# Seven block products for eight in the output projection of a fused attention and feed-forward kernel

## The chip, the cores and the metric

The kernel runs on one core of a Trainium2 chip. The metric is the device time of one execution in microseconds, from 2 runs of the kernel before: 248.40 and 248.44 us, median 248.42 us. Five engines work side by side, each with its own instruction queue that it executes in order: PE (TensorE, matrix products; its weight loads are listed apart as PEld), DVE (VectorE), ACT (ScalarE), POOL (GpSimd) and SP (SyncE, which here only issues DMAs). An instruction that needs another engine's result waits on a semaphore, and all that stands behind it in the queue of its engine waits with it. Matrix products are written to PSUM; PE, DVE and ACT work there, POOL works in SBUF only.

## The reference

There are 8 batches (`B`), 8 heads, 576 positions, head size 64, and 32 packed queries. First the packed queries attend to the keys and values, then the positions attend to the result; the outcome goes through a feed-forward layer whose activation is `h * cos(h)`:

```python
p_packed = sm_attn(p, k, v)
out = sm_attn(q, p_packed, p_packed)
x = attn_out.transpose(0, 2, 1, 3).reshape(B * S, H * D)    # 4608 x 512
h = x @ w_in                                                # 512 x 2048
g = h * np.cos(h)
return g @ w_out                                            # 2048 x 512, float32
```

`sm_attn` is a softmax attention. All products are taken in bf16 with fp32 sums in PSUM; `out` is fp32.

## The kernel before, in words

The program is written out by hand in one order for each engine; no planner moves anything. A tile pool hands out a free buffer when a tile is made in the program, and the first writer of the buffer waits until the last reader of its former tile has finished. Two PSUM pools matter: `psA` (three buffers of two banks, pool `A`) and `ot` (two buffers of one bank, pool `O`).

The work of batch s is split into a **front** and a **slot**.

- The front of s has the second attention of s: scores and their exponentials (`s2`), the second half of the product of the packed values and `w_in` (`ppw`, parts 2 and 3; DVE casts them from `psA` to the SBUF tile `PPW`), the softmax sums by a product with a block of ones (`sums2`, followed by a logarithm on ACT) and `normalise`, which takes the exponential of minus that logarithm on ACT and multiplies on DVE into the bf16 tile `a2n`. It has also the first scores of batch s+1 (`s1`).
- The slot of s makes the hidden layer in 16 steps (`h_mm(s, fc)`, fc = 0 to 15). Each step has four products of 288 columns on PE (L256) into a `psA` buffer, the cosine on ACT (L260) and the multiplication on DVE (L263), which writes 128 rows of `gT[s]`. At some steps hooks are called: `pp(s+1)` (L183) needs the permuted values `vp`, which POOL makes with one copy for each batch (`permute_v`), and `a1T`, which a transposing DMA on SP's queue brings; `pw2(s+1)` makes the first two parts of `PPW` of the next batch.
- Between all of this `fill(n)` puts n products of the **output projection of batch s-1**. Each product has one 128 x 128 block of `gT` as its weights and 512 columns of `w_out` (L309). 16 of them make a chunk of 128 positions in one `ot` buffer; a copy then brings it to SBUF (`osb`: on DVE in the fronts, on ACT in the slots) and SP issues its stores. 576 positions are four chunks and a half. The last 64 positions of two neighbouring batches are copied by POOL into the tile `joint` (L267) and make one more chunk. In the front of s, 32 products are put between the steps; the slot spreads the rest over its 16 steps and keeps 5 for the beginning of the next front.

Batches 0, 1 and 2 have fronts of their own (L366 to L505), and from 3 on there is one loop (L507). After the slot of batch 7, the output projection of batch 7 follows alone (L542, L543) and at last the joint chunk of batches 6 and 7 in two halves of 256 columns (`tail_chunk`, L295).

POOL's queue in the steady part of a batch has the two `joint` copies, `permute_v`, a tiny copy that waits for a transposed tile (`gate`, L527), and the issue of the loads of `v`, `q` and `k` of later batches. SP's queue has the stores of the chunks and the transposing DMAs of `q`, `a1` and `k`.

Of the kernel before, what the change touches and what calls it, by code (L numbers as in the profile page):

```python
# [8 lines left out]
FP32 = mybir.dt.float32  # L9
BF16 = mybir.dt.bfloat16  # L10
# [5 lines left out]
def kernel(  # L16
# [10 lines left out]
    nc = tc.nc  # L27
    B, H, S, D = q.shape
# [5 lines left out]
    TP = S // C  # L34
    HS = S // 2
# [4 lines left out]
    const = ctx.enter_context(tc.tile_pool(name="const", bufs=1))  # L40
    bf_pool = ctx.enter_context(tc.tile_pool(name="bf", bufs=1))
    vp_pool = ctx.enter_context(tc.tile_pool(name="vp", bufs=2))
    att_pool = ctx.enter_context(tc.tile_pool(name="att", bufs=1))
    a2n_pool = ctx.enter_context(tc.tile_pool(name="a2n", bufs=2))
    ppw_pool = ctx.enter_context(tc.tile_pool(name="ppw", bufs=2))
    g_pool = ctx.enter_context(tc.tile_pool(name="g", bufs=2))
    j_pool = ctx.enter_context(tc.tile_pool(name="joint", bufs=2))
    cos_pool = ctx.enter_context(tc.tile_pool(name="cos", bufs=3))
    o_pool = ctx.enter_context(tc.tile_pool(name="o", bufs=4))
# [8 lines left out]
    w_out_bf = const.tile([128, NFC, DM], BF16, name="w_out_bf")  # L58
    ident = const.tile([128, 128], BF16, name="ident")
# [3 lines left out]
    p_raw = const.tile([128, 2 * B, D], FP32, name="p_raw")  # L63
# [131 lines left out]
    def ppw(b, n, eng=None, own=False, later=False, cuts=((0, 512),)):  # L195
        if b not in PPW:
            PPW[b] = ppw_pool.tile([128, 2, DF], BF16, name="PPW", tag="PPW")
# [12 lines left out]
        def evacuate(cuts=cuts):  # L210
            if own or two:
                for a, z in cuts:
                    for y in range(2):
                        copy(eng[y] if two else eng, PPW[b][:, y, n * 512 + a:n * 512 + z], ps[y][:, a:z])
            else:
                copy(eng or (V, ACT)[n % 2], PPW[b][:, :, n * 512:(n + 1) * 512], t)
# [4 lines left out]
    def s2(b):  # L221
        a2u[b] = att_pool.tile([128, 2, S], BF16, name="a2u", tag="a2u")
# [5 lines left out]
    def sums2(b, y):  # L228
        if b not in lns:
            lns[b] = att_pool.tile([128, 2, S], FP32, name="lns", tag="lns")  # L230
        ps = psa()
        for e in range(2):
            nc.tensor.matmul(ps[:, e, 0:HS], ones_blk, a2u[b][:, y, e * HS:(e + 1) * HS],  # L233
                             start=True, stop=True)
        ACT.activation(out=lns[b][:, y].rearrange("p (e x) -> p e x", e=2),  # L235
                       in_=ps[:, :, 0:HS], func=AF.Ln)

    def normalise(b):
        a2n[b] = a2n_pool.tile([128, 2, S], BF16, name="a2n", tag="a2n")
        for y in range(2):  # L240
            ACT.activation(out=lns[b][:, y], in_=lns[b][:, y], func=AF.Exp, scale=-1.0)  # L241
        for y in range(2):
            V.scalar_tensor_tensor(out=a2n[b][:, y], in0=a2u[b][:, y], scalar=r1[b][:, y:y + 1],  # L243
# [331 lines left out]
```

The softmax here doesn't subtract the row's maximum and nothing guards it: scores larger than these inputs give would overflow.

## Time and profile before

| | |
|---|---|
| median of 2 runs | 248.42 us (248.40 to 248.44) |
| profiled execution, its own time | 248.62 us |
| its span, first to last instruction | 246.8 us |
| granted TensorE clock | 1.000 |
| PE, DVE, ACT, POOL busy | 233.2, 165.2, 169.0, 57.7 us |
| hidden layer on DVE (L263), 128 times | 93.8 us, 755 ns each |
| products of the output projection (L309), 128x512 | 127.5 us and 12.8 us (joint chunks) |
| DMA, mean | 151 GB/s, 37.36 MB in packets |

The span is 1.8 us shorter than the profiled execution's time, since a part of the start and the end lies outside the first and the last instruction. In the rows of groups the second number is the mean duration of one instruction. Products are pipelined on PE: the listed 379 ns of one product of 512 columns is from its first to its last effect, and the next one starts earlier; how many fit into a stretch is seen in the rows of the timeline, which merge instructions of one kind (start, duration, engine, line, operation, count).

### The profile page before, as it was taken

The numbers are of one execution on the slowest core, as the hardware profiler recorded it, in microseconds if no ns is written. First come the engines' busy times: TensorE is split into PE (matmuls) and PEld (weight loads), VectorE is DVE, ScalarE is ACT, GpSimd is POOL, SyncE is SP. The second block draws the span as 40 slices with busy tenths as digits, with TensorE's granted clock in tenths as the row PEclk, the third lists the DMA queues.
The fourth block names the chain that finished last, engine by engine and source line by source line (L and its number), as shares of the span: only waits on it lengthen the run. The fifth ranks groups of instructions, "written<-read, shape, count | busy, mean of one in ns | idle before, by whom it ended". The sixth has DMA issues, their size and how long they took to land.

```text
span 246.8 us, 5023 instructions
## 1 busy us (share of the span) xinstructions
PE 233.2 (94%) x1996; PEld 130.9 (53%) x2029; DVE 165.2 (67%) x248; ACT 169.0 (68%) x282; POOL 57.7 (23%) x70
## 2 busy tenths in 40 slices
PE   8788799999999999999999999999999999999993
PEld 3454374566545654565446554565456554665452
DVE  3549987677658776678767766678766684886110
ACT  2369799877576787888787776888778684873000
POOL 8342533240400355004503105030500100001000
PEclk9999999999999999999999999999999999999999
DMA  6999999999899999999999997999571113111133
GB/s 90 202 203 206 205 206 228 194 241 151 179 202 184 192 175 214 218 198 142 222 211 187 172 201 91 198 166 171 109 154 27 45 43 84 43 31 57 47 84 85
DMA packets 64231, 37.36 MB, mean 151 GB/s; under 512 B 36848, under 2 KB 59632, under 8 KB 64208
## 3 DMA queue, kind: packets, MB, share of 16 engines
q0 software_dynamic: 23152, 18.75, 50.0%
q1 hardware_dynamic: 40624, 18.09, 35.1%
q8 instruction: 16, 0.26, 0.4%
q10 hardware_dynamic: 432, 0.20, 0.4%
q14 instruction: 7, 0.06, 0.1%
HBM read 37.22 MB, written 9.44 MB: 189 GB/s over the span
## 4 chain that ended last, share of the span: by engine, by line
PE 78%; DMA 12%; issue 2%; DVE 2%; ACT 2%; POOL 2%; DVEq 0%; POOLq 0%
PE ot L309 46%; PE psA L256 21%; DMA vbf<-in_v_dram 10%; PE psA L207 3%; DMA a1T<-a 2%; PE psA L129 2%; PE psA L183 2%; DVE gT L263 2%; PE ot L295 1%; PE psA L233 1%; ACT cosT L260 1%; POOL vp L77 1%; ACT ppT L75 1%; POOL kbf L84 1%; PE ot L104 0%
## 5 line engine op out<-in xcount | busy, mean ns | idle before, releaser
L309 PE MATMUL ot<-w_out_bf,gT 128*128 128x512 bf16 x482 | 127.5, 379 | 2.0 <-issue 1.1
L263 DVE TENSOR_TENSOR gT<-psA,cosT 128x576 bf16<-128x576 f32 x128 | 93.8, 755 | 28.9 <-ACT cosT L260 28.2
L260 ACT ACTIVATE cosT<-psA 128x576 bf16<-128x576 f32 x128 | 82.4, 652 | 24.6 <-PE psA L256 22.1
L256 PE MATMUL psA<-a2n,PPW 128*128 128x288 bf16 x512 | 83.8, 286 | 1.6 <-DVE gT L263 0.4
L309 PEld LDWEIGHTS <-gT 128*128 128x128 bf16 x512 | 47.8, 98 | 43.4 <-issue 6.7
L256 PEld LDWEIGHTS <-PPW 128*128 128x128 bf16 x512 | 49.3, 98 | 34.6 <-issue 3.9
L77 DVE CAST PPW<-psA 128x1024 bf16<-128x1024 f32 (+1 forms) x23 | 26.9, 1175 | 11.6 <-PE psA L207 11.5
L267 POOL COPY joint<-gT 128x512 bf16<-128x512 bf16 x16 | 9.9, 616 | 82.5 <-DVE gT L263 82.5
L77 DVE COPY osb<-ot 128x512 f32<-128x512 f32 (+1 forms) x22 | 14.9, 678 | 17.5 <-PE ot L309 7.7
L77 POOL COPY vp<-vbf 96x3072 bf16<-96x3072 bf16 x7 | 19.3, 2751 | 6.3 <-DMA vbf<-in_v_dram 6.3
L75 ACT COPY osb<-ot 128x512 f32<-128x512 f32 (+1 forms) x15 | 8.5, 567 | 15.3 <-PE ot L309 10.6
L243 DVE SCALAR_TENSOR_TENSOR a2n<-a2u,r,lns 128x576 bf16<-128x576 bf16 x16 | 12.3, 812 | 7.3 <-ACT lns L241 7.3
L235 ACT ACTIVATE lns<-psA 128x576 f32<-128x576 f32 x16 | 10.1, 650 | 7.1 <-PE psA L233 6.5
L140 ACT ACTIVATE a<-psA 128x576 bf16<-128x576 f32 x16 | 10.3, 647 | 6.7 <-PE psA L129 6.7
L309 PE MATMUL ot<-w_out_bf,joint 128*128 128x512 bf16 x47 | 12.8, 379 | 0.1
L225 ACT ACTIVATE a2u<-psA,rs 128x576 bf16<-128x576 f32 x16 | 11.0, 737 | 1.4 <-PE psA L129 1.3
L75 ACT CAST ppT<-psA 64x128 bf16<-64x128 f32 x24 | 6.2, 260 | 7.0 <-DVE ppT L77 5.9
L207 PE MATMUL psA<-w_in_bf,ppT 64*32 64x512 bf16 x224 | 10.1, 380 | 0.0
L241 ACT ACTIVATE lns<-lns 128x576 f32<-128x576 f32 x16 | 10.0, 676 | 0.0
L347 PE MATMUL ot<-wz 128*128 128x512 bf16 x23 | 7.7, 468 | 1.4 <-DVE wz L358 1.2
L527 POOL COPY gate<-kT 1x1 bf16<-1x1 bf16 x3 | 0.5, 181 | 32.3 <-DMA kT<-kbf 32.3
L183 PEld LDWEIGHTS <-vp 96*128 96x128 bf16 x192 | 6.5, 98 | 2.3 <-issue 1.2
(73 smaller groups left out, 152.7 us busy)
## 6 DMA issues: line engine op xcount, KB each, us to landing
kbf<-in_k_dram POOLq DMA_DIRECT2D x8, 576.0 KB, 12.6
vbf<-in_v_dram POOLq DMA_DIRECT2D x8, 576.0 KB, 7.6
qbf<-in_q_dram POOLq DMA_DIRECT2D x8, 576.0 KB, 10.1
out_dram<-osb SPq DMA_DIRECT2D x24, 192.0 KB, 2.7
out_dram<-osb SPq DMA_DIRECT2D x22, 128.0 KB, 2.4
w_in_bf<-in_moe_w_in_dram POOLq DMA_DIRECT2D x4, 512.0 KB, 17.3
w_out_bf<-in_moe_w_out_dram POOLq DMA_DIRECT2D x4, 512.0 KB, 21.2
out_dram<-osb SPq DMA_DIRECT2D x26, 64.0 KB, 2.1
```

Source lines behind the costliest of these rows:

```text
L75: ACT.copy(out=out, in_=in_)
L77: eng.tensor_copy(out=out, in_=in_)
L140: ACT.activation(out=a1[b % 2][:, y, :, 0:TP].rearrange("p (e m) x -> p e m x", e=2), in_=ps[y][:, :, 0:HS].rearrange("p e (m x) -> p e m ...
L183: nc.tensor.matmul(ps[:, hp * 64:(hp + 1) * 64], vp[b][:, c, hp * 128:(hp + 1) * 128], a1T[b][0:TP, :, j, 32 * hp:32 * hp + 32], start=(j ...
L207: nc.tensor.matmul(ps[y][32 * x:32 * x + 32, :], ppT[b % 2][r, 2 * x + y, :], w_in_bf[r, x, n * 512:(n + 1) * 512], start=True, stop=True)
L225: ACT.activation(out=a2u[b][:, y].rearrange("p (e x) -> p e x", e=2), in_=ps[y][:, :, 0:HS], func=AF.Exp, scale=rs1[b][:, y:y + 1])
L235: ACT.activation(out=lns[b][:, y].rearrange("p (e x) -> p e x", e=2), in_=ps[:, :, 0:HS], func=AF.Ln)
L243: V.scalar_tensor_tensor(out=a2n[b][:, y], in0=a2u[b][:, y], scalar=r1[b][:, y:y + 1], in1=lns[b][:, y], op0=ALU.mult, op1=ALU.mult)
L256: nc.tensor.matmul(ps[:, e, 0:HS], PPW[b][:, y, fc * 128:(fc + 1) * 128], a2n[b][:, y, e * HS:(e + 1) * HS], start=(y == 0), stop=(y == 1))
L260: ACT.activation(out=csv, in_=ps[:, :, 0:HS], func=AF.Sin, bias=PI_HALF)
L263: V.tensor_tensor(out=gT[b][:, fc, :].rearrange("p (e x) -> p e x", e=2), in0=ps[:, :, 0:HS], in1=csv, op=ALU.mult)
L309: nc.tensor.matmul(pss[c], w, w_out_bf[:, fc, :], start=(fc == 0), stop=(fc == NFC - 1))
```

## The change

The output projection of batches 1 to 7 is made differently. Chunks 2 and 3 are made as before, one after the other, and now come first, in the fronts. Chunks 0 and 1, 256 positions together, are made as one block product of 2 x 2 blocks (`pair_gen`): the rows in two blocks of 128 positions, the inner dimension in two halves (even and odd steps fc), the columns in two halves of 256. The eight block products are replaced by seven, with sums of blocks ahead of and behind them (the scheme of Strassen and Winograd). Each of the seven has 8 products of 256 columns, so a pair has 56 products of 256 columns for 32 of 512.

- **Sums ahead.** Four sums of blocks of `w_out` (`T_sums`, made once, on POOL, in and after slot 1) and four sums of blocks of `gT` for each batch (`S_sums`, made in two halves of 4 steps, so 8 instructions of 128x512 elements). These stand on POOL's queue at the beginning of the front of s for batch s-1 (`close`), ahead of `permute_v(s+1)`; for batch 1 one half of them stands behind `permute_v(3)`, and for batch 7 they are on DVE.
- **Sums behind.** The seven products come in five groups, each in one `ot` buffer: (1), (2, 6), (7), (4, 5), (3). ACT or DVE copies the first to SBUF, and DVE makes five additions for each pair (`plus`), of 512, 256, 512, 256 and 256 columns, from PSUM and SBUF to SBUF.
- **Joint chunks** are made in halves of 256 columns; for batches 3 to 6 one half goes with each batch.
- `fill` counts in halves: a product of 256 columns is one, a product of 512 columns is two. A slot keeps 10 halves for the next front: the last two of products (4, 5) and the eight of product 3.
- **`normalise`** works in PSUM: `sums2` writes the logarithm back to its `psA` buffer, the exponential stays there too, and DVE reads it from there; the two buffers are held until then. From batch 2 on the two multiplications of `normalise` are not put at once: the first one comes after `fill(7)`, the second after `fill(3)` more.
- Room in SBUF: `vp` has one buffer for two, `PPW` four tiles of 512 columns for two of 2048, `p_raw` shares its place with the fourth sum of `w_out`, and the tile `lns` is gone.

```diff
-    vp_pool = ctx.enter_context(tc.tile_pool(name="vp", bufs=2))
+    vp_pool = ctx.enter_context(tc.tile_pool(name="vp", bufs=1))
-    ppw_pool = ctx.enter_context(tc.tile_pool(name="ppw", bufs=2))
+    ppw_pool = ctx.enter_context(tc.tile_pool(name="ppw", bufs=4))
+    u_pool = ctx.enter_context(tc.tile_pool(name="u", bufs=2))
+    T = [const.tile([128, 8, 256], BF16, name=f"T{i}") for i in range(3)]
...
     def sums2(b, y):
-        if b not in lns:
-            lns[b] = att_pool.tile([128, 2, S], FP32, name="lns", tag="lns")
-        ps = psa()
+        ps = lns[b, y] = psa()
...
-        ACT.activation(out=lns[b][:, y].rearrange("p (e x) -> p e x", e=2),
-                       in_=ps[:, :, 0:HS], func=AF.Ln)
+        ACT.activation(out=ps[:, :, 0:HS], in_=ps[:, :, 0:HS], func=AF.Ln)
...
+    def normalise(b, later=False):
+        a2n[b] = a2n_pool.tile([128, 2, SQ], BF16, name="a2n", tag="a2n")
+        for y in range(2):
+            t = lns[b, y][:, :, 0:HS]
+            ACT.activation(out=t, in_=t, func=AF.Exp, scale=-1.0)
+
+        def product(y):
+            v = [t[b][:, y].rearrange("p (e x) -> p e x", e=2) for t in (a2n, a2u)]
+            V.scalar_tensor_tensor(out=v[0], in0=v[1], scalar=r1[b][:, y:y + 1],
+                                   in1=lns[b, y][:, :, 0:HS], op0=ALU.mult, op1=ALU.mult)
+        if later:
+            return product
+        product(0)
+        product(1)
...
+    def A_blk(b, m, odd, k0, k1):
+        return gT[b][:, 2 * k0 + odd:2 * k1:2, m * 128:(m + 1) * 128]
+
+    def B_blk(odd, n):
+        return w_out_bf[:, odd:NFC:2, n * 256:(n + 1) * 256]
+
+    def T_sums(i, eng):
+        if i == 3:
+            T.append(s_pool.tile([128, 8, 256], BF16, name="T3", tag="x"))
+        in0, in1 = ((B_blk(0, 1), B_blk(0, 0)), (B_blk(1, 1), T[0]), (B_blk(1, 1), B_blk(0, 1)), (B_blk(1, 0), T[1]))[i]
+        eng.tensor_tensor(out=T[i], in0=in0, in1=in1, op=ALU.subtract)
...
+    def S_sums(b, p, eng, k0, k1, which=(0, 1, 2, 3)):
+        if (b, p) not in S:
+            S[b, p] = s_pool.tile([128, 4, 8, 128], BF16, name=f"S{p}", tag=f"S{p}")
+        t = S[b, p]
+        A11, A12 = (A_blk(b, 2 * p, i, k0, k1) for i in range(2))
+        A21, A22 = (A_blk(b, 2 * p + 1, i, k0, k1) for i in range(2))
+        S1, S2, S3, S4 = (t[:, i, k0:k1, :] for i in range(4))
+        for i in which:
+            out, in0, in1, op = ((S1, A21, A22, ALU.add), (S2, S1, A11, ALU.subtract),
+                                 (S3, A11, A21, ALU.subtract), (S4, A12, S2, ALU.subtract))[i]
+            eng.tensor_tensor(out=out, in0=in0, in1=in1, op=op)
...
+    def pair_gen(b, p):
...
+        A11, A12 = (A_blk(b, 2 * p, i, 0, 8) for i in range(2))
+        S1, S2, S3, S4 = (S[b, p][:, i] for i in range(4))
+        o1 = o_pool.tile([128, 3, 256], FP32, name="osb1", bufs=2)
+        o2 = o_pool.tile([128, 2, 256], FP32, name="osb")
+        m1, u3 = (u_pool.tile([128, 256], FP32, name=n, tag=n) for n in ("m1", "u3"))
+        m = {1: (A11, B_blk(0, 0)), 2: (A12, B_blk(1, 0)), 3: (S4, B_blk(1, 1)),
+             4: (A_blk(b, 2 * p + 1, 1, 0, 8), T[3]), 5: (S1, T[0]), 6: (S2, T[1]), 7: (S3, T[2])}
+
+        def then_double(ps):
+            plus(o2, ps, u3)
+            store(o2, 2 * p + 1)
+            plus(o1[:, 2], ps[:, 1], o1[:, 2])
+
+        def then_last(ps):
+            plus(o1[:, 1], ps, o1[:, 2])
+            store(o1, 2 * p)
+
+        then = {1: lambda ps: copy(out_eng[0], m1, ps), 2: lambda ps: plus(o1[:, 0:3:2, :], ps, m1),
+                7: lambda ps: plus(u3, ps, o1[:, 2]), 4: then_double, 3: then_last}
+
+        for names in ((1,), (2, 6), (7,), (4, 5), (3,)):
+            ps = O.tile([128, 2, 256], FP32, name="ot", tag="ot")
+            for i, n in enumerate(names):
+                lhs, rhs = m[n]
+                for kp in range(8):
+                    nc.tensor.matmul(ps[:, i], lhs[:, kp, :], rhs[:, kp, :], start=kp == 0, stop=kp == 7)
+                    if kp == 7 and n == names[-1]:
+                        then[names[0]](ps if i else ps[:, 0])
+                    yield 1
...
+    def out_gen(b):
+        for j, i in joints_of(b):
+            yield from joint_half(j, i, store_half(j))
+        if b == 0:
+            yield from direct_gen(b, ((0, 1), (2,), (3,)))
+        else:
+            yield from direct_gen(b, ((2,), (3,)))
+            yield from pair_gen(b, 0)
...
+    def close(s, groups=(0, 4)):
+        fill(1000)
+        for k0 in groups:
+            S_sums(s, 0, V if s == B - 1 else G, k0, k0 + 4)
+        set_filler(s)
...
-    slot(1, [(3, lambda: pw2(1, 2, (ACT, V))), (4, lambda: (xbar("q", 2), xbar("k", 3))), (5, tk("k", 2, 0)), (6, tk("k", 2, 1)),
-             (7, tk("k", 2, 2)), (9, lambda: pack_p(2, 4)), (12, next_loads)], 4, {3: 3})
+    slot(1, [(1, lambda: (T_sums(0, G), T_sums(1, G))), (3, lambda: pw2(1, 2, (ACT, V))), (4, lambda: (xbar("q", 2), xbar("k", 3))), (5, tk("k", 2, 0)), (6, tk("k", 2, 1)),
+             (7, tk("k", 2, 2)), (9, lambda: pack_p(2, 4)),
+             (12, next_loads)], 8, {3: 3})
+    T_sums(2, G)
+    T_sums(3, G)
...
-    fill(1000)
-    set_filler(1)
+    close(1, (0,))
...
-    normalise(2)
+    product = normalise(2, later=True)
     ACT.preload_act_table_set(SIN_SET)
-    fill(8)
+    fill(7)
+    product(0)
+    fill(3)
+    product(1)
     G.tensor_copy(out=gate, in_=a2n[2][0:1, 1, 0:1])
     permute_v(3)
+    S_sums(1, 0, G, 4, 8)
...
-        fill(1000)
-        set_filler(s - 1)
+        close(s - 1)
         if nxt:
             permute_v(s + 1)
...
-        normalise(s)
+        product = normalise(s, later=True)
         ACT.preload_act_table_set(SIN_SET)
-        fill(13)
+        fill(7)
+        product(0)
+        fill(3)
+        product(1)
+        fill(3)
...
-        slot(s, [(5, lambda: pp(s + 1, engs=(ACT, ACT))), (10, lambda: pw2(s + 1))] if nxt else [], 5, {10: 3})
-    out_eng[:] = V, ACT
-    set_filler(B - 1)
+        slot(s, [(5, lambda: pp(s + 1, engs=(ACT, ACT))), (10, lambda: pw2(s + 1))] if nxt else [], 10, {10: 3})
+    close(B - 1)
     fill(1000)
-    tail_chunk(B - 1, 4)
+    tail_chunk(B - 1)
```

## The prediction

> **What bounds the kernel now.** I read the page's busy shares and slices first, then the timeline of one batch, then the timeline of the places where the changed program holds a buffer longer. In the slices a 9 means 90% or more.
>
> ```profile
> PE 233.2 (94%) x1996; PEld 130.9 (53%) x2029; DVE 165.2 (67%) x248; ACT 169.0 (68%) x282; POOL 57.7 (23%) x70
> ...
> PE   8788799999999999999999999999999999999993
> ```
>
> From the seventh slice (some 37 us) on PE is full until the end. In a slot a step takes four products of L256 (0.49 us) and one or two of L309, and the next step follows at once: 129.86, 130.78, 131.70 for steps with two. So a product taken from PE there shortens the run by its full time, and every wait put ahead of PE lengthens it as directly, since PE's queue passes nothing.
>
> The rate of the two product sizes stands at the end of the timeline, where PE runs the last batch alone:
>
> ```profile
> 223.84 15.27 PE L309 MATMUL ot<-w_out_bf,gT 128*128 128x512 bf16 x69
> ...
> 239.16 3.66 PE L295 MATMUL ot<-w_out_bf,joint 128*128 128x256 bf16 x32
> ```
>
> From 223.84 to 239.16 are 71 products by the program (7 left over, 64 of batch 7; two records are missing): 215.8 ns each. The 32 of 256 columns take 3.66 us with 0.27 for the last one's full duration: (3.66 - 0.27)/31 = 109.3 ns. Half the columns cost half the time.
>
> **What goes from PE.** A pair of chunks was 32 x 215.8 = 6.91 us and becomes 56 x 109.3 = 6.12. Over 7 batches: -5.49 us. Three joint chunks become 32 x 109.3 for 16 x 215.8: +0.13. Net **-5.36 us**; the hidden layer and the attention keep their products.
>
> **What is added on DVE, and the price of its rows.** Per pair five additions from PSUM. The trace has no such addition; the nearest rows are the osb copy of 512 columns (690 ns), of 256 columns (424 ns), and the multiplication with one PSUM and one SBUF input of 576 columns (755 ns, 0.70 when back to back). I take 0.69 and 0.42: 2.6 us per pair, where before two ACT copies stood. A slot had 16 x 0.755 + 1.22 (cast of PPW) = 13.3 us of DVE in 15 to 19 us; only 1.1 us of the additions (2, 6 and 7) fall into it, so DVE isn't the bound by throughput. What counts is whom an addition keeps waiting.
>
> **(a) Front boundary.** One boundary in the timeline of before:
>
> ```profile
> 146.78 1.89 PE L309 MATMUL ot<-w_out_bf,joint 128*128 128x512 bf16 x8
> ...
> 147.66 0.76 DVE L263 TENSOR_TENSOR gT<-psA,cosT 128x576 bf16<-128x576 f32 x1 [0.16 <-ACT cosT L260]
> ...
> 148.70 0.69 DVE L77 COPY osb<-ot 128x512 f32<-128x512 f32 x1 [0.29 <-PE ot L309]
> ...
> 149.18 2.33 PE L309 MATMUL ot<-w_out_bf,gT 128*128 128x512 bf16 x9
> ```
>
> The last step's products end at 146.78 (call it t0). The last multiplication ends at t0 + 1.64. Before, the next chunk (149.18, t0 + 2.40) took the other `ot` buffer, long free. Now both are taken, by (4, 5) and (3). That of (4, 5) is free after two additions queued behind the last multiplication: 1.64 + 0.69 + 0.42 and some 0.05 for the semaphore = t0 + 2.80. PE gets there at 14 x 0.109 = 1.53, plus 0.68 for the scores and the part of `ppw` in between (148.50 to 149.18): t0 + 2.21. PE waits 0.6 us, ahead of fronts 3 to 7: **+3.0** (bounds: 0.3 each if the additions take half a copy, 0.9 if the slot ends with DVE late). Ahead of batch 7's own projection nothing covers: 2.80 - 1.53 = **+1.3**.
>
> **(b) Start of the slots.** The first step needs both halves of `a2n`.
>
> ```profile
> 154.48 2.97 PE L309 MATMUL ot<-w_out_bf,gT 128*128 128x512 bf16 x12
> ...
> 155.93 1.55 DVE L243 SCALAR_TENSOR_TENSOR a2n<-a2u,r,lns 128x576 bf16<-128x576 bf16 x2 [1.46 <-ACT lns L241]
> ...
> 157.28 0.65 PE L256 MATMUL psA<-a2n,PPW 128*128 128x288 bf16 x4
> ```
>
> `a2n` was whole at 157.48, PE came to the second half at 157.53: no slack at all. In the changed order of batches 4 to 7 (16 halves of a joint chunk first) chunk 2 ends 10 halves behind the last `sums2`, and its copy stands ahead of the first multiplication on DVE: 154.48 + 1.09 + 0.2 = 155.77, copy to 156.46, multiplications to 157.24 and 158.01. PE waits 0.5 to 0.6 there: **+2.2** for four batches (0 if DVE reads PSUM that much faster, 0.8 each if slower). In front 3 the copy falls elsewhere, and nothing is lost.
>
> **(c) `psA` held by `normalise`.** Two of the three buffers stay with the logarithms until the multiplications.
>
> ```profile
> 18.08 1.48 DVE L77 COPY kT<-psA 128x768 bf16<-128x768 bf16 x3 [1.40 <-PE psA L104]
> ...
> 19.49 1.53 DVE L243 SCALAR_TENSOR_TENSOR a2n<-a2u,r,lns 128x576 bf16<-128x576 bf16 x2
> ...
> 22.64 1.19 ACT L260 ACTIVATE cosT<-psA 128x576 bf16<-128x576 f32 x2
> ```
>
> At the start three groups of transposes (0.47 us each) filled three buffers; now they share one, each behind the copy of the one before: copies end at 18.6, 19.7, 20.9, the multiplications start 1.4 us later, and half of the scores of batch 1 wait for the first. The first cosine comes about 1.9 later. DVE has no gap up to 31.5 and then 0.53, 0.33 and 0.24 us of them to win back: **+0.8** (0 to 1.9). In front 2 two parts of `ppw` follow each other:
>
> ```profile
> 73.55 0.63 PE L207 MATMUL psA<-w_in_bf,ppT 64*32 64x512 bf16 x16
> ...
> 74.03 2.35 DVE L77 CAST PPW<-psA 128x1024 bf16<-128x1024 f32 x2 [1.16 <-PE psA L207]
> ```
>
> One free buffer: the second part waits for the first cast, 1.2 + 0.3 = 1.5 us on PE. The 0.38 us that PE waits for `a1T` at 84.43 goes: **+1.1** (0.7 to 1.9).
>
> **(d) Inside the slots** two additions stand between multiplications, and a `psA` buffer comes free up to 0.7 later. With steps of 0.85 us (62 halves in a slot) that is nearly covered: 0.1 each in slots 4 to 7; in slots 2 and 3 (48 and 46 halves, steps of 0.76, as long as a multiplication) 0.3 each: **+1.0** (0 to 4). **(e) The end:** (4, 5) waits 0.2 for the addition behind (2, 6), the last joint half 0.55 for the two behind (4, 5): **+0.75**.
>
> **(f) POOL.** No sum of two inputs by POOL is in the trace. Its copies of 512 and 3072 elements take 0.616 and 2.751 us: 0.19 + 0.834 ns per element. A sum of 512 costs 0.62 if the second input is free, 1.04 if it counts as one more element, 2.1 as upper end (twice that). I take 1.04, nearest to the copies.
>
> ```profile
> 148.48 0.61 POOL L267 COPY joint<-gT 128x512 bf16<-128x512 bf16 x1 [9.36 <-DVE gT L263]
> ...
> 149.03 2.75 POOL L77 COPY vp<-vbf 96x3072 bf16<-96x3072 bf16 x1
> ```
>
> Eight sums now stand between these two rows. `pp`, which needs `vp`, came at 161.80, 13.3 us behind the joint copy; with (a) and (b) 14.5. 0.61 + 8 x 1.04 + 2.75 = 11.7: in time. Above 1.39 us per sum `vp` is late. The sums of `w_out` (0.19 + 4096 x 0.834 ns = 3.6 us each) fit into POOL's waits of 9.1 and 9.6 us in slot 1 and front 2. Loads and the queue of SP shift by under 1 us: **0**. The last batch's sums on DVE (8 below 0.75) end ahead of product 6, 11 us behind t0.
>
> [...]
>
> **Sum.** -5.36 + 3.0 + 1.3 + 2.2 + 0.8 + 1.1 + 1.0 + 0.75 = **+4.8 us**. Profiled execution 248.62 + 4.8 = 253.4; it was 0.2 above the median, so **253.2 us**. 2% of 248.42 (5.0 us) is about what a measurement can tell from no change; this lies beside it.
>
> **Rivals.** *The waits are covered* (22%): the additions are short, products and multiplications slide into place, and of the losses only the two in (c) remain: 248.4 - 5.4 + 1.9 = 245; with half of (a), (b), (d), (e) 249. For it: DVE has a third of the span idle. Against it: each wait is a place in one queue, not a share. *POOL comes late* (15%): from 1.39 us per sum on, each 0.1 more makes `pp` wait 8 x 0.1 in fronts 3 to 6, 3.2 us in all; at 1.6 it is 6.7 us, 260; at 2.1 it is 23 us, 276. For it: two inputs through an engine which copies at 0.83 ns per element. Against: 23% busy. *The seven products don't run at half time* (8%) between products of 288 columns with other weights: at 120 ns for 109, 56 x 7 x 0.011 = 4.3 us, 257.5.
>
> **How the numbers follow.** My forecast (55%) runs from 249 to 257.5 with its terms' bounds. The range 246.5 to 259 leaves out the bottom of the first rival (8%) and the top of POOL's (11%). Faster by over 2% (below 243.4) needs all waits covered: 4%. Slower by over 2% (above 253.4) is the forecast's upper half and the last two rivals: 50%. Same: 46%.
>
> **What would show it.** Right: PE busy falls by about 5 us while its idle time grows by 10; PE waits of 0.6 us for DVE at the first `ot` product of fronts 3 to 7 and 1.3 ahead of batch 7; 0.5 at the start of slots 4 to 7; 1.5 in front 2; the first cosine near 24.5. Wrong: `pp` waiting for POOL's `vp`, POOL sums above 1.4 us, products of 256 above 112 ns, or PE full throughout.

## The result and the profile after

The changed kernel takes **257.88 us** (257.21 and 258.56) against 248.42 before: 1.038 times as long, with a 95% interval of 1.026 to 1.050. The profiled execution took 257.21 us, with a span of 255.4 us, 8.6 us more than before in both.

The page's lines on busy time and the slices, as they answer to those of the kernel before (PEclk is the granted clock of TensorE in tenths):

```profile
PE 233.0 (91%) x2226; PEld 153.2 (60%) x2245; DVE 185.7 (73%) x284; ACT 167.9 (66%) x285; POOL 127.6 (50%) x122
...
PE   8777589999997999999999999999999999998993
...
PEclk9999979999999999999999999999999999999999
```

PE has as much busy time as before, though its work fell by 5.4 us (reckoned from the rates of the two product sizes). The slices say where to look: a 5 in the fifth, followed by a sixth at a lower clock. That is stage 0, from 25 to 38 us. I call the moment at which a slot's last hidden-layer products end, and PE goes on to the next row of the timeline, the end of the slot. Its time, us, with the difference below:

| | slot 0 | slot 1 | slot 2 | slot 7 | span |
|---|---|---|---|---|---|
| before | 36.85 | 61.60 | 93.35 | 223.84 | 246.8 |
| after | 41.70 | 66.73 | 99.75 | 231.45 | 255.4 |
| later by | 4.85 | 5.13 | 6.40 | 7.61 | 8.6 |

More than half of the loss is there before the first slot ends, ahead of every block product. The rows of the timeline of the changed kernel in that place (start, duration, engine, line, operation, count, and in brackets the idle time before it and what ended it):

```profile
24.63 1.19 ACT L266 ACTIVATE cosT<-psA 128x576 bf16<-128x576 f32 x2
...
28.31 0.78 POOL L87 DMA_DIRECT2D kbf<-in_k_dram  x1 [1.87 <-DMA vbf<-in_v_dram]
...
28.77 3.10 DVE L155 TENSOR_SCALAR rs<-r 128x2 f32<-128x2 f32 x1
...
29.09 2.76 POOL L80 COPY vp<-vbf 96x3072 bf16<-96x3072 bf16 x1
...
32.58 1.93 PE L262 MATMUL psA<-a2n,PPW 128*128 128x288 bf16 x8 [2.94 <-DVE gT L269]
```

The first cosine comes at 24.63, 1.99 late. Then DVE spends 3.10 us on `rs`, the product of two numbers per partition with a constant, and its row ends with POOL's copy of `vp` (29.09 + 2.76 = 31.85). Behind `rs` stand the multiplications, PE's three `psA` buffers are full, and PE waits 2.94 us. Its clock falls after that, as the answer by stretches shows (length, busy time of PE, PEld, DVE, ACT and POOL with the instructions in brackets, granted clock, share and GB/s of the DMA engines):

```profile
30.00:32.00 2.00, 0.00 (x0) 0.00 (x0) 2.00 (x2) 0.42 (x1) 1.84 (x1) 1.00 1.32 205
32.00:34.00 2.00, 1.40 (x7) 0.62 (x7) 2.00 (x4) 0.65 (x1) 0.78 (x1) 0.82 1.25 207
34.00:36.00 2.00, 2.00 (x15) 0.77 (x14) 1.89 (x4) 1.17 (x2) 0.61 (x1) 0.50 1.24 205
36.00:38.00 2.00, 2.00 (x34) 1.61 (x33) 1.66 (x3) 1.58 (x4) 0.00 (x0) 0.83 1.24 206
```

At half clock PE counts as busy and gets less done: eight products of the hidden layer from 35.00 took 1.97 us, where eight from 30.70 took 1.16 before the change. So a lost 2.94 us became more, and the busy sum of PE hides it. In the groups by line, `rs` is a line that I had not read before:

```profile
L155 DVE TENSOR_SCALAR rs<-r 128x2 f32<-128x2 f32 x8 | 10.1, 1260 | 0.3
```

In the kernel before the same group (L152) had 1.8 us in 8 instructions, 231 ns each.

The waits that the prediction did name are there, all a little shorter. From timelines of the changed kernel: front 2, the front and the slot of batch 5, and the last batch.

```profile
80.94 0.41 PE L209 MATMUL psA<-w_in_bf,ppT 64*32 64x512 bf16 x8 [1.35 <-DVE PPW L80]
...
155.00 1.91 PE L322 MATMUL ot<-w_out_bf,joint 128*128 128x256 bf16 x16 [0.35 <-DVE osb L369]
...
163.77 0.41 PE L262 MATMUL psA<-a2n,PPW 128*128 128x288 bf16 x2 [0.26 <-DVE a2n L245]
...
234.08 7.08 PE L344 MATMUL ot<-w_out_bf,gT 128*128 128x512 bf16 x31 [0.94 <-DVE osb L369]
241.00 1.91 PE L396 MATMUL ot<-w_out_bf,gT 128*128 128x256 bf16 x16
242.74 1.91 PE L396 MATMUL ot<-T,S 128*128 128x256 bf16 x16
...
247.73 3.65 PE L322 MATMUL ot<-w_out_bf,joint 128*128 128x256 bf16 x32 [0.33 <-DVE osb L369]
```

The 16 products from 241.00 to 242.74 take 109 ns each. And POOL's sums, the first with 512 elements, the second (one of `w_out`) with 2048:

```profile
69.01 4.06 POOL L289 TENSOR_TENSOR T<-w_out_bf 128x2048 bf16<-128x2048 bf16 x1
...
78.28 1.15 POOL L303 TENSOR_TENSOR S<-S,gT 128x512 bf16<-128x512 bf16 x1
```

### The profile page after: what moved, and what is told of

Its sections match the earlier page's. It is cut to its first block, busy times and chain, and to the rows that moved or that the text cites. A ratio compares the mean times of both kernels' runs of the same rounds, so it can differ in the third digit from the quotient of the medians.

```text
span 255.4 us, 5593 instructions
## 1 busy us (share of the span) xinstructions
PE 233.0 (91%) x2226; PEld 153.2 (60%) x2245; DVE 185.7 (73%) x284; ACT 167.9 (66%) x285; POOL 127.6 (50%) x122
## 4 chain that ended last, share of the span: by engine, by line
PE 64%; DVE 16%; ACT 9%; issue 5%; DMA 4%; POOL 1%; DVEq 0%; ACTq 0%; POOLq 0%
PE ot L344 20%; PE psA L262 20%; PE ot L396 11%; DVE gT L269 6%; PE ot L322 5%; ACT cosT L266 5%; DMA qbf<-in_q_dram 4%; DVE osb L369 3%; DVE a2n L245 2%; PE psA L209 2%; ACT ppT L78 2%; PE psA L233 2%; PE psA L132 2%; DVE osb L80 1%; PE psA L107 1%
## 5 line engine op out<-in xcount | busy, mean ns | idle before, releaser
L344 PE MATMUL ot<-w_out_bf,gT 128*128 128x512 bf16 x271 | 70.2, 379 | 2.1 <-DVE osb L369 1.4
L303 POOL TENSOR_TENSOR S<-gT 128x512 bf16<-128x512 bf16 x24 | 27.7, 1152 | 0.0
L396 PE MATMUL ot<-T,S 128*128 128x256 bf16 x168 | 24.4, 273 | 0.0
L396 PEld LDWEIGHTS <-S 128*128 128x128 bf16 x224 | 21.5, 98 | 4.5 <-issue 1.4
L396 PE MATMUL ot<-w_out_bf,gT 128*128 128x256 bf16 x112 | 18.0, 273 | 0.0
L322 PE MATMUL ot<-w_out_bf,joint 128*128 128x256 bf16 x128 | 15.4, 272 | 1.8 <-DVE osb L369 1.8
L235 ACT ACTIVATE psA<-psA 128x576 f32<-128x576 f32 x16 | 10.0, 635 | 7.8 <-PE psA L233 3.8
L322 PEld LDWEIGHTS <-joint 128*128 128x128 bf16 x128 | 12.2, 98 | 4.8 <-issue 3.5
L303 POOL TENSOR_TENSOR S<-S,gT 128x512 bf16<-128x512 bf16 x12 | 13.8, 1151 | 0.9
L303 POOL TENSOR_TENSOR S<-gT,S 128x512 bf16<-128x512 bf16 x12 | 13.8, 1154 | 0.0
```

The costliest lines, as they stand in the source:

```text
L235: ACT.activation(out=ps[:, :, 0:HS], in_=ps[:, :, 0:HS], func=AF.Ln)
L303: eng.tensor_tensor(out=out, in0=in0, in1=in1, op=op)
L322: nc.tensor.matmul(ps, joint[b // 2][:, fc, :], w_out_bf[:, fc, cols], start=(fc == 0), stop=(fc == NFC - 1))
L344: nc.tensor.matmul(pss[c], gT[b][:, fc, c * 128:(c + 1) * 128], w_out_bf[:, fc, :], start=(fc == 0), stop=(fc == NFC - 1))
L396: nc.tensor.matmul(ps[:, i], lhs[:, kp, :], rhs[:, kp, :], start=kp == 0, stop=kp == 7)
```

## The experiments

Every kernel was timed against the kernel before on the same chip. All ends of slots are from the one profiled execution of each. Kernels 1 to 4, 5 to 8, 9 and 10, 11 and 12 shared a chip; between these groups the ratios are the safer comparison. The changed kernel itself has two runs, 1.35 us apart.

| kernel | median, us | ratio to before (95%) | slot 0 | slot 2 | slot 7 | span |
|---|---|---|---|---|---|---|
| 1 `rs` on ACT | 256.31 | 1.0305 (1.026 to 1.035) | 37.16 | 98.19 | 229.90 | 253.9 |
| 2 first logarithms in SBUF | 262.10 | 1.0532 (1.049 to 1.058) | 37.10 | 102.84 | 234.53 | 258.5 |
| 3 products direct | 256.00 | 1.0300 (1.027 to 1.034) | 41.17 | 98.86 | 230.69 | 253.8 |
| 4 before, `rs` later | 250.90 | 1.0095 (1.006 to 1.013) | 38.18 | 94.16 | 224.64 | 247.6 |
| 5 `rs` on ACT, joint later | 252.75 | 1.0189 (1.016 to 1.022) | 37.39 | 95.12 | 226.82 | 250.8 |
| 6 joint later alone | 256.26 | 1.0326 (1.030 to 1.035) | 40.70 | 98.37 | 230.09 | 254.1 |
| 7 all waits mended | 251.43 | 1.0123 (1.010 to 1.015) | 37.97 | 94.38 | 227.59 | 249.7 |
| 8 as 7, products direct | 249.87 | 1.0044 (1.001 to 1.007) | 37.09 | 93.81 | 225.18 | 247.2 |
| 9 as 7, shorter fronts | 249.10 | 1.0005 (0.999 to 1.002) | 38.20 | 94.62 | 224.27 | 247.3 |
| 10 as 7, fewer additions | 249.53 | 1.0031 (1.001 to 1.005) | 37.66 | 93.98 | 225.34 | 247.4 |
| 11 as 9, products direct | 249.92 | 1.0052 (1.003 to 1.007) | 38.28 | 94.95 | 226.32 | 248.3 |
| 12 as 9, start and end mended | 248.50 | 0.9985 (0.997 to 1.000) | 37.13 | 93.58 | 223.73 | 246.8 |

### 1 to 4: is it the tiny instruction, and do the products bring anything?

**Experiment 1**, the changed kernel with `rs` on ACT, in `s2(b)` ahead of its exponentials:

```diff
-        V.tensor_scalar(out=rs1[b], in0=r1[b], scalar1=scale, scalar2=None, op0=ALU.mult)
...
+        ACT.activation(out=rs1[b], in_=r1[b], func=AF.Copy, scale=scale)
```

> The changed kernel, but the tiny product rs = scale x r (128x2 elements, on DVE in recips) is made on ACT, just ahead of the exponentials that use it; nothing else moves. Theory L (lock): in batch 0 DVE's rs row of 3.10 us is a wait for POOL's instructions of the same moment (the issue of the load at 28.31 and the copy vp at 29.09 to 31.85), so with rs gone from DVE the PE gap of 2.94 us and the stretch of half clock behind it go too, and stage 0 ends 3 to 4 us earlier: 253 to 254.5 us. Theory H (held buffers): the late start alone, psA held by the logarithms, puts the loss there, and the rs row only shows when DVE would have waited anyhow: within 0.7 us of the changed kernel, 256.7 to 258.5. ACT has 8 more instructions of some 0.2 us, both theories count them at nothing.

Stage 0 did what theory L said: slot 0 ended at 37.16, 4.5 us earlier, 0.3 later than before the change. The run did not: 256.31, 1.6 less than the changed kernel and above L's range. Between slot 0 and slot 2 it lost 3 us again. POOL's and PE's timelines of this kernel:

```profile
64.90 0.18 POOL L547 COPY gate<-kT 1x1 bf16<-1x1 bf16 x1 [1.08 <-DMA kT<-kbf]
65.42 0.79 POOL L87 DMA_DIRECT2D qbf<-in_q_dram  x1 [0.34 <-issue]
66.20 0.77 POOL L87 DMA_DIRECT2D kbf<-in_k_dram  x1
66.96 0.77 POOL L87 DMA_DIRECT2D vbf<-in_v_dram  x1
67.73 0.62 POOL L273 COPY joint<-gT 128x512 bf16<-128x512 bf16 x1
```

```profile
64.18 1.05 PE L322 MATMUL ot<-w_out_bf,joint 128*128 128x256 bf16 x8
68.40 0.39 PE L322 MATMUL ot<-w_out_bf,joint 128*128 128x256 bf16 x2 [3.17 <-POOL joint L273]
```

The second `joint` copy of slot 1 stands in POOL's queue behind three loads, and these behind a tiny copy that waits for a transposed tile until 64.9. Before the change this copy ended at much the same time (67.73 + 0.62) and nobody needed it: the joint chunk was the last of batch 1. The change makes the joint halves the first, so PE stands ahead of their ninth product. In the changed kernel PE came to the halves only at 68.49 and did not wait: the late start hid it.

**Experiment 2**, the changed kernel with the logarithms of batch 0 in SBUF:

```diff
+        if b == 0:
+            if y == 0:
+                lns[b] = s_pool.tile([128, 2, 2, HS], FP32, name="lns0", tag="S0")
+            lns[b, y] = lns[b][:, y]
-        ACT.activation(out=ps[:, :, 0:HS], in_=ps[:, :, 0:HS], func=AF.Ln)
+        ACT.activation(out=lns[b, y][:, :, 0:HS], in_=ps[:, :, 0:HS], func=AF.Ln)
```

> The changed kernel, but batch 0 alone writes its logarithms to an SBUF tile again, so that psA is not held at the start; rs stays on DVE. Theory L with the start: the three groups of transposes of k run in three buffers, the first cosine comes near 22.6 (not 24.63), rs falls at 26.8 ahead of POOL's vp copy and takes 0.2 us; the end of slot 0 comes 4 to 5 us earlier: 252.4 to 253.5 us. Rival: the start is 2 us earlier but the run gains only these 2 us or less, because the rest of the loss has another source in stage 0: 255 to 256.5 us.

Both were wrong about the run: 262.1, slower than the changed kernel. At the start all went as expected (`rs` at 27.02 in 0.17 us, slot 0 ended at 37.10). Then came the wait for `joint` (3.24 us), and in front 2 `rs` met POOL again, now a sum of `w_out`. From DVE's, POOL's and PE's timelines of this kernel:

```profile
71.28 4.88 DVE L155 TENSOR_SCALAR rs<-r 128x2 f32<-128x2 f32 x1
```

```profile
72.09 4.05 POOL L293 TENSOR_TENSOR T<-w_out_bf,T 128x2048 bf16<-128x2048 bf16 x1
```

```profile
76.55 0.59 PE L348 MATMUL ot<-w_out_bf,gT 128*128 128x512 bf16 x2 [2.55 <-DVE osb L80]
```

`rs` began 0.8 ahead of this sum, while the one before it was running (68.08 to 72.13), and ended with the second (76.14). The copies of the output stood behind it, and PE waited 2.55 us more; from 68.6 to 72.0, behind the wait for `joint`, the granted clock was 0.50. In the changed kernel the same row in front 2 took 1.40 us and stopped nobody. So an earlier start was worth 4.6 us in stage 0 and cost 7.7 in the two stages after it (65.74 us from slot 0 to slot 2, for 58.05 in the changed kernel and 56.50 before).

**Experiment 3**, the block products alone undone (`pair_gen`, `S_sums` and `T_sums` not called):

```diff
-            yield from direct_gen(b, ((2,), (3,)))
-            yield from pair_gen(b, 0)
+            yield from direct_gen(b, ((2,), (3,), (0,), (1,)))
```

> The changed kernel with the block products undone alone: chunks 0 and 1 of batches 1 to 7 as 32 products of 512 columns each pair, behind chunks 2 and 3, no sums on POOL or DVE; logarithms in PSUM, late multiplications, joint halves and buffers stay as changed. If the seven products bring their 5.5 us of PE time nearly whole, and the losses lie in what stays: 261 to 263 us. If the additions of the pairs take back what the products give (waits of 0.4 at five front boundaries, 0.9 ahead of batch 7, 0.3 at the end and delays inside the slots): 255 to 257.5 us.

256.00, the second theory. From slot 2 to slot 7 direct products took 131.83 us and block products 131.70: 3.9 us less of PE's work (5 pairs of 0.79) moved this stretch by 0.1. What remains after this edit, over 3% above the kernel before, is none of the products' doing: the held `psA` with `rs` behind it, the wait in front 2, the slot starts.

**Experiment 4**, the kernel *before* with `recips(1)` three steps later and nothing else:

```diff
-        if fc == 3:
+        if fc == 6:
             recips(1)
```

> The kernel before with one move: the two tiny DVE instructions of batch 1 (r and rs, 128x2 elements each) stand three steps later in batch 0's slot (behind step 6 in place of step 3), so that rs meets POOL's vp copy (29.13 to 31.89 in the profile of before). Nothing else of the change is in it. Theory L: the rs row grows from 0.17 to about 2.2 us and ends with POOL's copy; DVE has gaps of 1.1 us behind it to win back, so the run is 1.3 to 2.4 us longer: 249.7 to 250.8 us, more if PE's gap lowers its clock. Rival: an instruction of 128x2 costs 0.17 us wherever it stands, 248.2 to 248.7 us.

250.90, 0.95% slower: theory L, 0.1 us above its range. From DVE's, POOL's and PE's timelines of this kernel:

```profile
29.55 2.53 DVE L152 TENSOR_SCALAR rs<-r 128x2 f32<-128x2 f32 x1
```

```profile
29.29 2.75 POOL L77 COPY vp<-vbf 96x3072 bf16<-96x3072 bf16 x1
```

```profile
32.79 0.65 PE L256 MATMUL psA<-a2n,PPW 128*128 128x288 bf16 x4 [1.42 <-DVE gT L263]
```

The same instruction, 0.17 us at step 3, takes 2.53 at step 6 and ends 0.04 behind POOL's copy. Its neighbour `r` (a reciprocal of the same two numbers, 0.15) was not held up. Slot 0 ended 1.33 later in the profile. The ten times of this kernel lie from 249.15 to 252.47, wider than those of the kernel before, and follow the granted clock: three runs at 0.997 to 1.000 took 249.15 to 249.44 us, four at 0.985 or 0.986 took 252.04 to 252.47. So the row by itself costs some 0.7 us of the run, and some 3 more come with a lower clock.

In the rows of experiments 2 and 4 `rs`, an instruction of two elements per partition, ends just behind an instruction of POOL: at 76.16, where the sum ends at 76.14, and at 32.08, where the copy ends at 32.04. By what means POOL holds it up, no run here shows. When it gets in is not clear either: in experiment 2 `rs` ended with the second of two sums in a row, in front 2 of the changed kernel with the first (71.69 + 1.40 = 73.09; the sums stand at 69.01 to 73.07 and from 73.03).

The issue of a load on POOL may hold `rs` up too. In the changed kernel it did not end between 28.77 and 29.09, although no copy had begun. The trace of before has one row that points the same way; from DVE's and POOL's timelines:

```profile
26.77 0.17 DVE L152 TENSOR_SCALAR rs<-r 128x2 f32<-128x2 f32 x1
66.56 0.67 DVE L152 TENSOR_SCALAR rs<-r 128x2 f32<-128x2 f32 x1
```

```profile
29.13 2.76 POOL L77 COPY vp<-vbf 96x3072 bf16<-96x3072 bf16 x1
66.21 0.77 POOL L84 DMA_DIRECT2D kbf<-in_k_dram  x1
66.97 0.77 POOL L84 DMA_DIRECT2D vbf<-in_v_dram  x1
```

Beside two issues it took 0.67 us, and ended 0.26 behind the beginning of the second. But at 12.26 of the same trace it kept its 0.17 beside such issues (11.52 to 13.07), so this is not shown.

### 5 to 8: taking the waits away

**Experiment 5** is experiment 1 with the joint halves of batch 1 behind its chunks 2 and 3, **experiment 6** has this order alone:

```diff
-        for j, i in joints_of(b):
-            yield from joint_half(j, i, store_half(j))
+        halves = [joint_half(j, i, store_half(j)) for j, i in joints_of(b)]
+        if b != 1:
+            for g in halves:
+                yield from g
...
             yield from direct_gen(b, ((2,), (3,)))
+            if b == 1:
+                for g in halves:
+                    yield from g
             yield from pair_gen(b, 0)
```

> The changed kernel with rs on ACT, as in the first experiment, and one thing more: in the output projection of batch 1 the two joint halves stand behind chunks 2 and 3, not ahead of them. Theory T (two delays that hide each other): with rs off DVE stage 0 ended 4.5 us earlier, but PE then stood 3.17 us in front 2 ahead of the joint half, because POOL's joint copy is queued behind the issue of three loads, and these behind a tiny copy that waits for a transposed tile until 64.9. The late start of the changed kernel hid this. With both taken away: 252.5 to 253.8 us, 3 below the first experiment. Rival: the wait moves on to the next thing that POOL delivers or to the block sums of batch 1, and nothing or at most 1 us is gained on the first experiment: 255.3 to 256.5 us.

> The changed kernel with only the joint halves of batch 1 moved behind chunks 2 and 3; rs stays on DVE. Theory T: PE reaches the joint halves late enough in the changed kernel (68.49, no wait in the rows), so this alone brings nothing: 257 to 258.5 us. Rival: the joint copy costs the changed kernel something by itself, 254 to 255.5 us.

252.75 for both together, as theory T said; 256.26 for the order alone, which is between T and its rival. In the profile of experiment 6, 1.0 of the 1.3 us that the span is shorter is in stage 0, which the edit doesn't touch: `rs` there began at 30.42, late in POOL's copy, and took 1.59 instead of 3.10, with half clock from 21 to 28 instead of from 33 to 37. From slot 0 to slot 2 it gained 0.4. By the medians each edit alone brought 1.6 and both 5.1 (by the spans 1.5, 1.3 and 4.6): the two delays lay side by side.

**Experiment 7** adds what else was found. The two multiplications of `normalise` stand at once; the last part of `PPW` of batch 2 comes behind them; a slot keeps 20 halves (slots 2 and 3 as before 10, slot 7 none). **Experiment 8** is the same with direct products.

```diff
-    ppw(2, 3, V)
     product = normalise(2, later=True)
...
     product(1)
+    ppw(2, 3, V)
...
-        fill(7)
         product(0)
-        fill(3)
         product(1)
-        fill(3)
+        fill(13)
...
-        slot(s, [(5, lambda: pp(s + 1, engs=(ACT, ACT))), (10, lambda: pw2(s + 1))] if nxt else [], 10, {10: 3})
+        slot(s, [(5, lambda: pp(s + 1, engs=(ACT, ACT))), (10, lambda: pw2(s + 1))] if nxt else [], {3: 10, 7: 0}.get(s, 20), {10: 3})
```

> Every wait that was found is taken away, the seven products stay: rs on ACT, joint halves of batch 1 behind its chunks 2 and 3, the two multiplications of normalise at once in batches 3 to 7, the last part of PPW of batch 2 behind the multiplications, and 20 halves in place of 10 kept for the fronts of 5, 6 and 7 (10 for the front of 4, none ahead of batch 7's own projection). Sum from the rows: 252.5 to 253.8 of the kernel with rs on ACT and the order mended, less 1.35 (front 2), less 1.0 (slot starts), less 3 x 0.35 (fronts), less 1 (batch 7): 247.5 to 249.5 us. If the additions on DVE only wait elsewhere (PE kept up inside the slots): 251 to 253 us.

> The kernel with every found wait taken away, but with chunks 0 and 1 made directly, 32 products of 512 columns for each pair, and no block sums on any engine. It tells what the seven products bring when nothing else is in their way. If their 5.5 us of PE time arrive: 4.5 to 5.5 us above that kernel, 252 to 255 us. If additions on DVE inside the slots take half of it back even then: 2 to 3.5 us above it. If they bring nothing: within 1 us of it.

251.43 with the seven products, in the range of "the additions only wait elsewhere"; 249.87 without them. So with the named waits gone, eight products were 1.6 us *faster* than seven, which none of the three theories had. The answers by stretches for the stage of batch 5 (from the end of slot 4 to the end of slot 5), of experiment 7 and of experiment 8:

```profile
146.35:173.27 26.92, 26.11 (x260) 17.98 (x260) 19.90 (x30) 20.88 (x36) 14.66 (x14) 1.00 0.97 172
```

```profile
144.55:171.27 26.72, 26.41 (x234) 15.56 (x236) 18.59 (x26) 20.93 (x37) 5.63 (x6) 1.00 0.96 178
```

With seven products PE is idle for 0.81 us of the stage, with eight for 0.31. One gap is in the list of waits (0.56, `psA` held until a multiplication was done); the others are below 0.2 each. In experiment 7 the slot of batch 5 has 8 products of 512 columns and 33 of 256, in experiment 8 it has 28 of 512; with 0.49 us for the four products of each of 16 steps, 0.215 and 0.109 for these, 0.72 for `pp` and 0.58 for `ppw` that is 14.5 us of PE's work against 15.2 (the expectation of experiment 9 takes 14.3). The slots took 15.6 and 15.3.

### 9 to 12: the floor of a slot

That gave theory F: the steps of a slot have a floor, set by the cosine on ACT (0.65 us per step), the multiplication on DVE (0.755) and the copies between them, and the shortened output projection fell below it. Experiment 9 moves work from the front, where PE is the bound, into the slot; experiment 10 takes additions out of DVE's queue in the slot.

```diff
-        fill(10)
+        fill(6)
         if nxt:
             s1(s + 1)
```

> The kernel with every found wait taken away (seven products, 251.4 us), with one number changed: in the fronts of batches 3 to 7 six products of the output projection stand ahead of the scores of the next batch in place of ten, so four move from each front into its slot. Theory F (floor of the slot): the seven products made PE's work in a slot shorter than what ACT and DVE need for its 16 steps (14.3 us of PE work in the slot of batch 6, which took 15.6), so the time given back by PE is lost in short gaps; with four products more the slot is as long as with direct products, and the front is 0.86 us shorter. Gain 0.6 to 0.9 us for each of five batches, 247 to 248.5 us. Rival: the fronts are bound by the chain of exponentials and not by PE, and wait instead: 250.5 to 252 us.

```diff
-            plus(o2, ps, u3)
+            plus(o2, ps, m1)
...
-        then = {1: lambda ps: copy(out_eng[0], m1, ps), 2: lambda ps: plus(o1[:, 0:3:2, :], ps, m1),
-                7: lambda ps: plus(u3, ps, o1[:, 2]), 4: then_double, 3: then_last}
+        then = {1: lambda ps: copy(out_eng[0], m1, ps), 2: lambda ps: None,
+                7: lambda ps: None, 4: then_double, 3: then_last}
```

> The same kernel without the two additions of each pair that fall into the slot (behind products 2 and 6, and behind 7); the later additions take the copy of product 1 in their place, so part of the sums of chunks 0 and 1 is left out. Rival of theory F: the additions in DVE's queue hold the multiplications of the hidden layer back; without these 1.1 us for each batch on DVE the slots are 0.5 to 0.8 us shorter, 247.5 to 249 us. Theory F: without them the 16 steps are still bound by cosines, multiplications and the copies of ACT; at most 0.3 us for each slot, 250 to 251.4 us.

From slot 2 to slot 7, experiment 7 took 133.21 us, experiment 9 129.65, experiment 10 131.36. One number in the program was worth 3.56 us there, 0.71 per batch; 0.9 of it went again as a wait ahead of batch 7's projection (0.99 for 0.17), so that the median fell by 2.3 to 249.10 (2.9 by the ratios). The additions were worth 0.37 per slot, between the two expectations: they are a part of what holds the slot, not all of it. The stage of batch 5 in experiment 9:

```profile
145.36:171.28 25.92, 25.82 (x260) 17.99 (x260) 19.86 (x30) 20.81 (x37) 14.65 (x14) 1.00 1.06 184
```

One microsecond shorter than in experiment 7 with the same instructions, and PE idle for 0.10. The slot in it, first of experiment 7, then of experiment 9:

```profile
157.65:173.27 15.62, 15.00 (x145) 11.09 (x145) 12.44 (x18) 12.82 (x23) 5.66 (x6) 1.00 1.01 173
```

```profile
155.92:171.28 15.36, 15.31 (x148) 11.39 (x148) 12.29 (x18) 12.72 (x23) 6.51 (x7) 1.00 1.07 175
```

The front ahead of it fell from 11.30 to 10.56 us, and the slot, with 0.8 us more of PE's work, from 15.62 to 15.36, now full with 15.2 of work. So what theory F says of PE holds (the slots had room for these products), but 15.6 us was no fixed floor, and no engine alone sets one: in that slot of experiment 7 ACT was busy for 12.8 us and DVE for 12.4. The time went in waits along the chain of product, cosine, multiplication and free `psA` buffer. The wait of 0.56 us is there in experiment 10 too, without the additions, and gone in experiment 9; which link of the chain makes it was not taken apart.

**Experiment 11** is experiment 9 with direct products, **experiment 12** is experiment 9 with the first logarithms in SBUF (as in experiment 2) and, for batch 7, ten products ahead and its slot filled evenly.

```diff
-        fill(6)
+        fill(6 if nxt else 10)
...
-        slot(s, [(5, lambda: pp(s + 1, engs=(ACT, ACT))), (10, lambda: pw2(s + 1))] if nxt else [], {3: 10, 7: 0}.get(s, 20), {10: 3})
+        slot(s, [(5, lambda: pp(s + 1, engs=(ACT, ACT))), (10, lambda: pw2(s + 1))] if nxt else [], {3: 10, 7: 0}.get(s, 20), {10: 3} if nxt else {})
```

> The kernel with direct products for chunks 0 and 1 and every found wait taken away (249.9 us), with the same four products moved from each front of batches 3 to 7 into its slot as in the run before. Theory F: with direct products PE already sets the length of the slot, so moving work between front and slot changes nothing: 249 to 250.5 us, and the seven products then bring 0.5 to 1.5 us where the slot is long enough, far from 5.5. Rival: the move alone is what helps, products or not: 247 to 248 us.

> The best kernel with seven products so far (249.1 us) with two more edits: batch 0 writes its logarithms to SBUF, so that psA is free at the start (the end of slot 0 was 37.1 in the experiment with that edit, 38.2 in the best kernel), and batch 7 keeps ten products ahead and spreads the rest of its slot evenly, since PE stood 0.60 us in that slot and 0.99 us ahead of its own projection. Expected 0.5 to 1.5 us less, 247.6 to 248.6 us, so no more than 0.3% below the kernel before. If these waits only move on: 248.8 to 249.4 us.

249.92 for direct products: the move does nothing for them (249.87 without it), as theory F says. Against 249.10 the seven products now bring 0.8 us (1.2 by the ratios), and the intervals of the two ratios to the kernel before do not meet. The stage of batch 5 is 25.92 against 26.64: 0.72, nearly the whole 0.79 of a pair. The last version has 248.50 us, 0.15% below the kernel before, with an interval that ends just under 1: the best of all kernels here, by a hair. Its gain is at the start (slot 0 ended 1.07 earlier than in experiment 9), but not because the first cosine comes earlier: experiments 1 and 8, without that edit and at full clock, end slot 0 at 37.16 and 37.09. What is missing in experiment 12 is a stretch of half clock, from 22.2 to 25.6 in the profile of experiment 9 (by the rows: the first eight products of the hidden layer took 1.94 us there, from 23.97, and 1.14 in experiment 12, from 22.37). Its twelve runs had a granted clock of 0.996 or more, six of the ten of experiment 9 had 0.990 to 0.993; that the edit prevents the stretch fits this and was not tested by itself. The wait ahead of batch 7 stayed at 0.99, against the expectation, and `pp` of slot 3 waited 1.53 us (0.29 in experiment 9), of which I can't say why.

## Why the prediction came out as it did

The forecast was 253.2, slower, within 246.5 to 259.0; it is 257.88. The direction was right, and most of the named waits stood where they were forecast. That the time lies within the range is luck: more than half of the loss, 4.85 us of 8.6, is in a stage to which 0.8 was given, from a cause that the prediction did not have, and 257.88 lies above the forecast's own bounds (249 to 257.5), in a part of the range that was meant for two of the rivals, which did not happen. By stages, predicted and measured in the profiled executions:

| stage | predicted | measured |
|---|---|---|
| to the end of slot 0 | +0.8 | +4.85 |
| slot 1 | 0 | +0.28 |
| front 2 and slot 2 | +0.65 | +1.27 |
| fronts and slots 3 to 7 | +2.1 | +1.21 |
| the end | +1.3 | +1.0 |

(The pairs' 0.79 is put to the stage in which each is made.)

- **What goes from PE**: right as a rate (109 ns per product of 256), wrong as a gain. Products taken from a slot shorten the run only as far as its chain of 16 steps on ACT and DVE lets them. The prediction's sentence "a product taken from PE there shortens the run by its full time" is refuted by experiments 3, 7, 8 and 9. The sign "PE busy falls by about 5 us" didn't come either (233.2 and 233.0). A product of 256 columns is listed with 273 ns and the next one starts after 109, so a gap of up to 0.16 us behind it counts as busy, and half clock adds to it.
- **(a), (b), the additions' price**: right in place, each smaller. 682 and 420 ns (0.69 and 0.42 taken); 1.95 us in fronts 3 to 7 (3.0), 0.94 ahead of batch 7 (1.3), 1.0 at four slot starts (2.2).
- **(c)** is the step that failed. The part on front 2 was right: 1.35 (1.5). At the start, "first cosine about 1.9 later" was right (1.99), and so was "gaps to win back": with `rs` off DVE only 0.3 remain. What failed is that nothing but DVE's own queue was looked at. Two microseconds later `rs` no longer stood ahead of POOL's copy but beside it. It became 3.10, PE's gap 2.94, then half clock: 4.85 for 0.8. The row of 0.17 us in the trace of before was at 26.77, POOL's copy at 29.13; that they would meet could have been read from these two rows. That meeting costs something had one hint in the trace of before, the 0.67 us at 66.56 beside two issues of loads (seen in the group's mean, 231 ns for 0.17); it has no row of `rs` beside a POOL copy or sum, so the size could not be read.
- **(d)** was mis-sized and hid it in the sum: what the named waits leave over in slots 2 to 7 is 3.1 us, not 1.0. (Slots 3 to 7: 1.21 + 3.84 of PE's work, less 1.95 and 1.0 of waits, is 2.1; front 2 and slot 2 likewise 1.0.) The smaller waits in (a) and (b) made up for it, so the stages behind slot 1 fit by two errors.
- **(e)**: 0.33 for the joint half (0.55), none ahead of (4, 5).
- **(f)**: POOL was in time, `pp` never waited for `vp`. 1.15 us per sum, above the 1.04 taken and below the 1.39 at which `vp` would have been late; the sums of `w_out` 4.06, not 3.6. "Loads shift by under 1 us: 0" was right about the loads and missed who stands behind them: the `joint` copy, which the changed order needs 20 us sooner (the products of this joint chunk began at 88.63 before and begin at 68.49). In the changed kernel itself this cost nothing, since the start was late; it is 3.2 us as soon as that is mended.
- **Rivals**: not the waits covered, not POOL late, not the products' rate. The outcome, 4.7 us above the forecast's own number, came from something none of them named.

## What to carry to other kernels

When a step moves, look at every engine that its instructions will newly run beside, not only at their own queue: two numbers per partition cost 3.10 us here, for 0.17, when they met a GpSimd copy of 2.76. A delay that is found may cover another one: mending one of two that lie side by side brought 1.6 us, mending both 5.1, and mending the wrong one made it slower. And work saved on a full engine counts only as far as the other engines' chain in that stage lets it (3.9 us of it moved five stages by 0.1 in experiment 3); before shortening a step, put its other engines' times beside it, and take the saved work out where that engine alone is the bound.

## What the runs showed of the hardware

- A 128x2 `tensor_scalar` on DVE: 0.17 us alone (26.77 in the kernel before). Begun while a GpSimd copy or sum ran, it ended 0.01 to 0.04 us behind the end of a GpSimd instruction: in the changed kernel in six rows of 1.06 to 1.40 us and, begun before the copy, in the one of 3.10, in experiment 3 (2.07 us), in experiment 4 (2.53) and in experiment 2 (4.88), there behind the second one. The one exception began 0.07 us before a copy ended and kept its 0.17 (67.85 in experiment 4, where seven of the eight rows took 0.17). DVE's multiplications with an input in PSUM kept their 754 to 756 ns in all kernels, with GpSimd busy for 23% of the span in the kernel before and for 50% in the changed one.
- TensorE's granted clock fell to 0.50 behind an idle time of 2.94 us in the changed kernel, of 3.24 in experiment 2 and of 1.92 in experiment 3, and stayed at 1.00 behind one of 3.17 us in experiment 1 and of 1.42 in experiment 4. In experiment 6 two gaps of 0.65 us at the start, among small transposes, were followed by half clock; in the changed kernel the same gaps were not. By the mean clocks of the stretches of 2 us, the time at half clock behind these gaps was 3.4 us long in the changed kernel and in experiments 2 and 3, and 6.8, twice that, in experiment 6. How much idle time is enough no run here shows: gaps of one length had both outcomes.
